# Linear attention and an MLP in one kernel: v in whole rows, x sums on another engine, and two transposes moved to DMA

## The chip, the cores and the metric

The kernel runs on one core of a Trainium2 chip. The metric is the device time in microseconds (us), the median of the runs.

## The reference

For 8 batches, 8 heads, 576 tokens and a head size of 64, the kernel computes a linear attention and, on its result, a normalised MLP with a residual:

```
q_s = softmax(q over the head size);  k_s = softmax(k over the tokens)
kv  = k_s^T v                       (64 x 64 per head)
x   = q_s kv, heads side by side    (8 x 576 x 512)
xn  = (x - mean) / sqrt(var + 1e-6) * g
out = x + relu(xn w1) w2            (w1 512 x 2048, w2 2048 x 512)
```

Inputs and output are float32.

## The kernel before, in words

**Chunks.** The tokens are worked in nine chunks of 512. Chunks 0 to 7 are the first 512 tokens of each batch; chunk 8 (C9) gathers the last 64 of all batches. Within a chunk a partition holds four consecutive tokens (T = 4), so "token 2" of a chunk means the third of each partition, a tile of 128 tokens. All matrix operands are bf16.

**Order.** The order of the work is written by hand. `mlp_steps` gives a chunk's MLP as a list of single matmuls with weights: 1 for one of 512 columns, 0.5 for one of 256. `run` goes through it and puts in side work (the next chunk's attention, the loads, the sums) at positions counted in these weights; a chunk from 2 on has 112. An engine runs its own instructions strictly in that order, and semaphores join the engines. SyncE (SP) issues the loads of q and k and the DMA transposes, GpSimd (POOL) those of v and the stores.

**Attention of a chunk.** ScalarE takes exp of q and k (L171 to L203). q's result is transposed by DMA (`eq_T`, L253; batch 1's on TensorE, L864). `kv_all` (L321) multiplies exp(k) with v, 32 matmuls for the first 512 tokens and 8 for the rest, and `kv_out` scales the result on VectorE (L330, L332). v stands in `vm`, one buffer for even and one for odd batches, with a column of ones beside each head. `load_v` brings v of batches 1 to 3 as one DMA in rows of four tokens into the tile `vt`, from which VectorE copies it into `vm` (`cast_v`, L131, in two halves); for batches 4 to 7 four DMAs go straight into `vm`, one per token (L144). Then `po_mm` (L358) makes x for one token tile, `x_fast` on VectorE scales it (L388) and centres it into xn (L380), and ScalarE sums the squares (L372).

**xn turned.** For the MLP, xn has to be transposed: by DMA in two halves of two tokens (`xn_T`, L253), in chunks 0 and 1 on TensorE (`xn_pT`, L864) with a copy on ScalarE (L866) or VectorE (L868).

**MLP.** Chunk 0 and chunk 1's first matrix product are plain matmuls (L456 for parts of a chunk, L441 for a whole one, L501 for the second product). Everything after uses Strassen's scheme with seven products in place of eight, for which sums have to be made: of w1 and w2 once, of xn per chunk (`sum_x`, L245; on GpSimd, but on VectorE for chunk 8 and for one sum of chunk 7), and of the hidden layer (`sum_h`, L532, on VectorE, four sums in two halves). The first product (`mm1_fast`, L693) does four groups, two at a time. Of each, the products come in the order 1, 5, 6, 2, 7, 3, 4, each first for the one group and then for the other. ScalarE seeds bank c from bank x after product 1 (L717) and copies bank b to `s` after product 5 (L721); VectorE adds x and s into b after product 6 (L724), and adds x and s into the hidden layer after product 7 (L727), from the bank x to which product 4 then adds. The second product (`mm2_fast`, L548) has seven products of 16 matmuls; VectorE gives the output (L559; plain chunks L472), GpSimd stores it (L565).

**Positions.** In chunks 2 to 6 the first half of the first three h sums stand at 30, 33 and 41: the adds L724 of the second pair of groups come at 40, L727 at 48.

Of the kernel before, what the change touches and what calls it, by code (L numbers as in the profile page):

```python
# [20 lines left out]
def kernel(  # L21
# [16 lines left out]
    nc = tc.nc  # L38
# [13 lines left out]
    VW = D + 1  # L52
    C9 = B
    FAST = 1
    CAST = (1, 2, 3)
    T0 = S // 64
    assert SR == 64 and B % 2 == 0 and S % 64 == 0

# [67 lines left out]

    vts = {}

    def cast_v(b, j):
        hs = slice(4 * j, 4 * j + 4)  # L130
        nc.vector.tensor_copy(  # L131
            out=vm[:, b % 2, :, hs, 0:D].rearrange("p t h d -> p h t d"), in_=vts[b][:, hs]
        )

    def load_v(b):

        if b in CAST:
            vts[b] = mlp.tile([P, H, T, D], BF16, tag="tq", name="vt", bufs=1)
            nc.gpsimd.dma_start(
                vts[b].rearrange("p h t d -> p h (t d)"), main_src(v, b, 0, H)  # L140
            )
        src = v[b, :, 0:SM, :].rearrange("h (p t) d -> p t h d", t=T)
        for t in range(0 if b in CAST else T):
            nc.gpsimd.dma_start(vm[:, b % 2, t, :, 0:D], src[:, t])  # L144
        for half in range(2):
            hs = slice(4 * half, 4 * half + 4)
            nc.gpsimd.dma_start(
                vr[SR * half : SR * half + SR, b % 2, hs, 0:D],
                v[b, hs, SM:S, :].transpose([1, 0, 2]),
            )  # L150
# [82 lines left out]
    def sum_x(c, i):  # L233

        if i == 0:
            tqs[c] = mlp.tile([P, 4, 2, 2, P], BF16, tag="tq", name="tq", bufs=1)
        (b11, b12), (b21, b22) = [
            [xnTs[c][:, 2 * half : 2 * half + 2, 2 * kh : 2 * kh + 2, :] for half in range(2)]
            for kh in range(2)
        ]  # L240
        t1, t2, t3, t4 = [tqs[c][:, n] for n in range(4)]
        dst, x, y = ((t1, b12, b11), (t2, b22, t1), (t3, b22, b12), (t4, b21, t2))[i]
        eng = nc.vector if c == C9 or (c == C9 - 1 and i == 1) else nc.gpsimd
        for t in range(2):
            eng.tensor_tensor(out=dst[:, t], in0=x[:, t], in1=y[:, t], op=ALU.subtract)  # L245

# [201 lines left out]
    def mm1_part(c, m, t0, tn, ko):  # L448

        if (m, t0, ko) == (0, 0, 0):  # L450
            new_h()
        half, at = divmod(t0, 2)
        if m % 2 == 0 and at == 0 and ko == 0:
            hbox["ph", m // 2] = mm_ps.tile([P, 2, 2, P], FP32, tag="m", name="ph")
        ph = hbox["ph", m // 2]
        nc.tensor.matmul(  # L456
            ph[:, m % 2, at : at + tn], (w1g if c else w1_sb)[:, ko, m * P : (m + 1) * P],
            xnTs[c][:, t0 : t0 + tn, ko, :],
            start=(ko == 0), stop=(ko == KO1 - 1),
        )  # L460
        if m % 2 == 1 and at + tn == 2 and ko == KO1 - 1:
            dst = hbox["h"][:, m - 1 : m + 1, 2 * half : 2 * half + 2]
            if c == 0 and half and (m // 2) % 2 == 1:
                nc.vector.tensor_scalar_max(dst, in0=ph, scalar1=0.0)
            else:
                nc.scalar.activation(dst, ph, AF.Relu)
# [283 lines left out]
    def mlp_steps(c):  # L750
        if c > FAST:
            return mm1_fast(c) + mm2_fast(c)
        full = range(KO2)
        first, parts = [], ()
        if c == 0:
            full = range(0)
            parts = ((0, 2, 0, 1), (0, 2, 1, 1), (2, 2, 0, 1), (2, 2, 1, 1), (4, 4, 0, 2), (0, 4, 2, 1),
                     (0, 4, 3, 1), (4, 4, 2, 2), (8, 4, 0, 2), (8, 4, 2, 2), (12, 4, 0, 2), (12, 4, 2, 2))
        else:
            full, parts = range(8, KO2), ((0, 8, 0, 2), (0, 8, 2, 2))  # L760
        for m0, mn, t0, tn in parts:
            first += [
                (0.25 * tn, lambda m=m, t0=t0, tn=tn, ko=ko: mm1_part(c, m, t0, tn, ko))
                for m in range(m0, m0 + mn) for ko in range(KO1)
            ]
        first += [(1, lambda m=m, ko=ko: mm1(c, m, ko)) for m in full for ko in range(KO1)]
        if c == 0:
            return first + [
                (1, lambda t=t, ko=ko: mm2_stream(c, t, ko))
                for n in range(4) for t in range(T) for ko in range(4 * n, 4 * n + 4)  # L770
            ]
        if c >= FAST:
            return first + mm2_fast(c)
        return first + [(1, lambda t=t, ko=ko: mm2(c, t, ko)) for t in range(T) for ko in range(KO2)]
# [25 lines left out]
    def prep_fast(b):  # L800

        s = [(57, lambda: exp_q(b, 0, 4)), (65, lambda: exp_q(b, 2, 4)), (79, lambda: eq_T(b))]
        s += [(81, lambda: exp_k(b, 0, 4)), (98, lambda: exp_k(b, 2, 4))]
        s += [(106, lambda: prep_kvrem(b))]
        return s

    def recip_q(c):
# [2 lines left out]
    def attn_fast(c):  # L810

        s = [(1, lambda: reduce_q(c, 0, 2)), (27, lambda: reduce_q(c, 2, 2)), (28, lambda: recip_q(c))]
        s += [(12, lambda: kv_all(c))]
        s += [(40, lambda: start_x(c))]
        for t, (p0, p1) in enumerate(((48, 53), (57, 59), (65, 67), (73, 75))):
            s += spread([lambda t=t, i=i: po_mm(c, t, i) for i in range(NP)], p0, p1)
            s += [(p1, lambda t=t: x_fast(c, t)), ((66, 74, 87, 91)[t], lambda t=t: square_sum(c, t))]
        s += [(61, lambda: xn_T(c, 0, 2)), (78, lambda: xn_T(c, 2, 2)), (95, lambda: rstd_op(c))]
        s += [((84, 100 if c == C9 - 1 else 88, 92, 101)[i], lambda i=i: sum_x(c, i)) for i in range(4)]
        return s  # L820

    def second_side():

        s = [(p, lambda i=i: quarter_w2(i, 1)) for i, p in enumerate((8.5, 13, 44, 46))]
        s += [(8.0, lambda: xn_pT(1, 3, nc.vector))]
        s += [(3, lambda: exp_q(2, 0, 4)), (7, lambda: exp_q(2, 2, 4)), (7.2, lambda: eq_T(2))]
        s += [(42, lambda: square_sum(1, 2)), (67, lambda: square_sum(1, 3)), (71, lambda: rstd_op(1))]
        s += [(7.3, lambda: load_batch(3, (2,), eqTs[2][0:1, T - 1, NP - 1, 0:4])), (31, lambda: load_batch(3, (0,)))]
        s += [(9 + 2 * j, lambda j=j: cast_v(2, j)) for j in range(2)]
        s += [(7.4, lambda: load_v(3))]  # L830
        s += [(93 + j, lambda j=j: cast_v(3, j)) for j in range(2)]
        s += [(15 + 3 * t, lambda t=t: reduce_q(2, t, 2)) for t in (0, 2)]
        s += [(36, lambda: recip_q(2))]
        s += [(18, lambda: exp_k(2, 0, 4)), (22, lambda: exp_k(2, 2, 4)), (26, lambda: prep_kvrem(2))]
        s += [(41, lambda: kv_all(2))]
        s += [(46, lambda: start_x(2))]
        for t, (p0, p1) in enumerate(((52, 54), (57, 59), (62, 65), (70, 74))):
            s += spread([lambda t=t, i=i: po_mm(2, t, i) for i in range(NP)], p0, p1)
            s += [(p1, lambda t=t: x_fast(2, t)), ((73, 82, 88, 94)[t], lambda t=t: square_sum(2, t))]
        s += [(60, lambda: xn_T(2, 0, 2)), (77, lambda: xn_T(2, 2, 2)), (100, lambda: rstd_op(2))]  # L840
        s += [(75, lambda: exp_q(3, 0, 4)), (79, lambda: exp_q(3, 2, 4)), (85, lambda: eq_T(3))]
        s += [(97, lambda: exp_k(3, 0, 4)), (108, lambda: exp_k(3, 2, 4)), (113, lambda: prep_kvrem(3))]
        s += [(p, lambda i=i: sum_w1(i, 1)) for i, p in ((3, 30),)]
        s += spread([lambda i=i: sum_x(2, i) for i in range(4)], 95, 108)
        return s
# [184 lines left out]
    with tc.manual_schedule(  # L1030
# [10 lines left out]
        def po_x(c, t):  # L1041
# [26 lines left out]
            + [(p, lambda i=i: sum_w1(i, 1)) for i, p in enumerate((96, 98, 100))]  # L1068
            + [(103 + 0.4 * j, lambda j=j: cast_v(1, j)) for j in range(2)]
            + [(104.5, lambda: prep_kvrem(1))]  # L1070
            + [(105, lambda: kv_mm(1, range(T))), (106, lambda: (kv_mm(1, range(T, T + 1)), kv_out(1), start_x(1)))]
            + [(111, lambda: po_x(1, 0)), (113, lambda: po_x(1, 1))]
            + [(116, lambda: po_x(1, 2)), (118, lambda: xn_pT(1, 0, nc.scalar)), (119, lambda: square_sum(1, 0))]
            + [(119.5, lambda: po_x(1, 3)), (123, lambda: xn_pT(1, 1, nc.scalar)), (124, lambda: square_sum(1, 1))]
            + [(128, lambda: xn_pT(1, 2, nc.scalar))]

        )
        for c in range(1, B):
# [12 lines left out]
            if c == B - 2:  # L1091
                side += [(1, load_qrem)]
                side += spread([lambda r=r: exp_qrem(r) for r in range(T)], 58, 80)
                side += [(84, lambda: eq_T(C9))]
            sums = [(57, 0)] if c == FAST else [(p, i) for i, p in enumerate((30, 41) if c == B - 1 else (30, 33, 41))]
            run(mlp_steps(c), side + [(at, lambda i=i: sum_h(0, i)) for at, i in sums])
        run(mlp_steps(C9), [(33 + 3 * i, lambda i=i: sum_h(0, i)) for i in range(2)])

# [29 lines left out]
```

## Time and profile before

| | us |
|---|---|
| runs | 266.63, 266.06, 266.3; median 266.3 |
| the profiled execution's own time | 266.63 |
| its span, first to last instruction | 264.8 |
| busy: TensorE, VectorE, ScalarE, GpSimd | 257.6, 217.0, 175.1, 90.4 |

The 1.8 us between the execution's time and its span lie outside the instructions. A chunk from 2 on takes some 26.3 us: chunk 3 begins its first product at 103.7, chunk 4 at 130.1, chunk 5 at 156.5, chunk 6 at 183.2, chunk 7 at 209.4 (timeline of TensorE). In a timeline line stand the start, the time until the last end, the engine, the line and operation, the tiles written and read, their sizes and how many instructions are drawn together; in square brackets the idle time ahead of it and who ended it. Ends of matmuls are modelled, and some instructions overlap on their engine, so the starts say more than the durations. A few records are missing: a jump of just one matmul in the starts is no wait.

### The profile page before, as it was taken

To read this page: it belongs to the slowest core of one execution; us is meant where nothing else is said; L and a number is where in the kernel's file an instruction comes from. 1 tells how busy PE (TensorE), PEld (TensorE's weight loads), DVE (VectorE), ACT (ScalarE), POOL (GpSimd) and SP (SyncE) were. 2 spreads that over 40 slices of the span, in tenths; PEclk is the share of its full clock that TensorE was granted. 3 is DMA by queue.
4 is the path that set the end of the run, shared out by engine and by line. 5 is a ranking of instruction groups with operands and counts; after the bars stand their busy time and mean duration, and the time that the engine had idled before them with its cause. 6 is when DMAs were issued, how large, how long until landed. Compare 5 with 4: busy or idle time off the path is not lost. (4 is left out here: it accounts for less than half of the span.)

```text
span 264.8 us, 6827 instructions
## 1 busy us (share of the span) xinstructions
PE 257.6 (97%) x2708; PEld 217.5 (82%) x2711; DVE 217.0 (82%) x465; ACT 175.1 (66%) x346; POOL 90.4 (34%) x144
## 2 busy tenths in 40 slices
PE   8999999999999999999999999999999999999993
PEld 5778755775988998889888988998899888888882
DVE  4577697968989996999699968996999789877873
ACT  4467851996966886678667866886678378438400
POOL 8742216303059208900880049307300800030000
PEclk9999999999999999999999999999999999999999
DMA  7999999987987995899789997997804530512014
GB/s 226 252 205 207 342 209 329 262 132 255 184 149 221 291 139 101 222 286 143 98 243 268 125 113 235 294 126 155 257 5 84 120 118 5 78 80 81 0 42 119
DMA packets 82328, 45.01 MB, mean 170 GB/s; under 512 B 58036, under 2 KB 78520, under 8 KB 82296
## 3 DMA queue, kind: packets, MB, share of 16 engines
q0 software_dynamic: 32800, 22.29, 45.8%
q1 hardware_dynamic: 48896, 21.76, 40.5%
q10 hardware_dynamic: 600, 0.53, 0.6%
q8 instruction: 21, 0.34, 0.5%
q14 instruction: 11, 0.09, 0.1%
HBM read 36.70 MB, written 9.44 MB: 174 GB/s over the span
## 5 line engine op out<-in xcount | busy, mean ns | idle before, releaser
L548 PEld LDWEIGHTS <-hs 128*128 128x128 bf16 x512 | 49.5, 98 | 5.7
L693 PEld LDWEIGHTS <-w_q 128*128 128x128 bf16 x448 | 43.0, 98 | 6.4 <-issue 1.1
L245 POOL TENSOR_TENSOR tq<-xnT 128x256 bf16<-128x256 bf16 x24 | 15.6, 665 | 76.6 <-DMA xnT<-xn 76.6
L548 PEld LDWEIGHTS <-hT 128*128 128x128 bf16 x384 | 37.2, 98 | 4.4
L693 PEld LDWEIGHTS <-w1g 128*128 128x128 bf16 x336 | 32.2, 98 | 3.9
L548 PE MATMUL ba<-w_q,hs 128*128 128x256 bf16 x256 | 31.7, 273 | 0.0
L693 PE MATMUL bx<-tq,w_q 128*128 128x256 bf16 x224 | 29.4, 272 | 0.2 <-ACT s L721 0.2
L372 ACT ACTIVATE scrap<-x,mv 128x512 bf16<-128x512 bf16 x36 | 25.9, 719 | 1.7 <-DVE x L388 1.3
L717 ACT COPY bc<-bx 128x512 f32<-128x512 f32 x28 | 15.2, 594 | 16.8 <-PE bx L693 16.8
L388 DVE SCALAR_TENSOR_TENSOR x<-po,rq 128x512 bf16<-128x512 f32 x34 | 23.3, 685 | 2.4 <-PE po L358 2.3
L565 POOL DMA_DIRECT2D out_dram<-ot x28 | 15.4, 556 | 24.1 <-DVE ot L559 24.0
L735 ACT ACTIVATE hT<-bc 128x512 bf16<-128x512 f32 x28 | 15.3, 595 | 12.4 <-PE bc L693 12.4
L207 DVE TENSOR_REDUCE zq<-eq 128x16 f32<-128x1024 bf16 (+1 forms) x20 | 20.6, 1049 | 2.0 <-ACT eq L198 2.0
L532 DVE TENSOR_TENSOR hs<-hT 128x1024 bf16<-128x1024 bf16 x32 | 21.3, 674 | 0.9 <-ACT hT L735 0.5
L724 DVE TENSOR_TENSOR bb<-bx,s 128x512 f32<-128x512 f32 x28 | 18.2, 694 | 4.1 <-ACT s L721 4.0
L735 ACT ACTIVATE hT<-bb 128x512 bf16<-128x512 f32 x28 | 15.2, 595 | 9.2 <-PE bb L693 9.2
L358 PE MATMUL po<-kv_sb,eqT 128*128 128x128 bf16 x120 | 20.5, 219 | 0.0
L727 DVE TENSOR_TENSOR hT<-bx,s 128x512 bf16<-128x512 f32 x28 | 18.0, 685 | 2.8 <-PE bx L693 2.8
L573 ACT COPY s<-ba 128x512 f32<-128x512 f32 x15 | 8.7, 579 | 12.5 <-PE ba L548 7.8
L548 PE MATMUL ba<-w_sb,hT 128*128 128x256 bf16 x128 | 16.7, 273 | 0.0
L548 PE MATMUL bb<-w_q,hs 128*128 128x256 bf16 x128 | 16.6, 273 | 0.0
L501 PE MATMUL pc<-w_sb,hT 128*128 128x512 bf16 x61 | 15.8, 379 | 0.2
(135 smaller groups left out, 541.1 us busy)
## 6 DMA issues: line engine op xcount, KB each, us to landing
out_dram<-ot POOLq DMA_DIRECT2D x32, 256.0 KB, 5.6
qt<-in_q_dram SPq DMA_DIRECT2D x5, 1024.0 KB, 6.3
kt<-in_k_dram SPq DMA_DIRECT2D x5, 1024.0 KB, 12.8
w_sb<-in_moe_w_ch_dram POOLq DMA_DIRECT2D x4, 512.0 KB, 16.4
qt<-in_q_dram POOLq DMA_DIRECT2D x2, 1024.0 KB, 14.6
kt<-in_k_dram POOLq DMA_DIRECT2D x2, 1024.0 KB, 14.5
vm<-in_v_dram POOLq DMA_DIRECT2D x16, 128.0 KB, 13.2
w_raw<-in_moe_w_ch_dram POOLq DMA_DIRECT2D x3, 512.0 KB, 12.8
```

Source lines behind the costliest of these rows:

```text
L207: nc.vector.reduce_sum(eqs[c][1][:, ts], eqs[c][0][:, ts], axis=AX.X)
L245: eng.tensor_tensor(out=dst[:, t], in0=x[:, t], in1=y[:, t], op=ALU.subtract)
L358: nc.tensor.matmul(pobox["p"][:, i * P : i * P + P], eqTs[c][:, t, i, :], kv_sb[:, c, i, :], start=True, stop=True,)
L372: nc.scalar.activation(scrap, x[:, t], AF.Square, bias=mv[:, t, 0:1], scale=-float(DM), accum_out=mv[:, t, 1:2],)
L388: nc.vector.scalar_tensor_tensor(x[:, t].rearrange("p (h d) -> p h d", h=H), in0=pobox[c, t].rearrange("p (h d) -> p h d", h=H), scalar=1. ...
L501: nc.tensor.matmul(hbox["pc", t], hbox["h"][:, ko, t, :], w2_sb[:, ko, :], start=(ko == 0), stop=(ko == KO2 - 1),)
L532: nc.vector.tensor_tensor(out=dst, in0=x, in1=y, op=op)
L548: nc.tensor.matmul(hbox[bank][:, t], lhsT, rhs, start=first and (own or t == 0) and k == 0, stop=k == KH - 1, skip_group_check=True)
L693: nc.tensor.matmul(dst[:, q], lhsT, rhs, start=first and q == 0 and ko == 0, stop=ko == 1, skip_group_check=True)
L724: nc.vector.tensor_tensor(out=at[g, "b"], in0=at[g, "x"], in1=at[g, "s"], op=ALU.add)
L727: nc.vector.tensor_tensor(out=h_out(g, 1, 1), in0=at[g, "x"], in1=at[g, "s"], op=ALU.add)
L735: nc.scalar.activation(h_out(g, odd, half), at[g, name], AF.Relu)
```

## The change

v of every batch from 1 on is now loaded as one DMA into `vt`, which has a buffer of its own (before, it shared one with the x sums). For batches 4 to 7 VectorE copies the first half into `vm` at position 94.5 and ScalarE the second at 107, in the chunk two before their own. All x sums of chunk 7 are on VectorE, at position 100. In chunk 1, tokens 2 and 3 of xn are transposed by DMA at chunk 0's position 125, and no longer on TensorE; for this x of token 3 comes ahead of the output of token 1, and the first product works 12 of 16 blocks of hidden columns on tokens 0 and 1 alone, before it takes up tokens 2 and 3 (before: 8 of 16). The kv product of batch 1 is no longer split around a matmul and stands at 106. In chunks 2 to 6 the h sums move from 30, 33, 41 to 30, 40.5, 42.

```diff
-    CAST = (1, 2, 3)
...
-    def cast_v(b, j):
+    def cast_v(b, j, eng=None):
         hs = slice(4 * j, 4 * j + 4)
+        dst = vm[:, b % 2, :, hs, 0:D].rearrange("p t h d -> p h t d")
+        if eng is nc.scalar:
+            nc.scalar.copy(dst, vts[b][:, hs])
+        else:
+            nc.vector.tensor_copy(out=dst, in_=vts[b][:, hs])
...
     def load_v(b):
-        if b in CAST:
-            vts[b] = mlp.tile([P, H, T, D], BF16, tag="tq", name="vt", bufs=1)
-            nc.gpsimd.dma_start(
-                vts[b].rearrange("p h t d -> p h (t d)"), main_src(v, b, 0, H)
-            )
-        src = v[b, :, 0:SM, :].rearrange("h (p t) d -> p t h d", t=T)
-        for t in range(0 if b in CAST else T):
-            nc.gpsimd.dma_start(vm[:, b % 2, t, :, 0:D], src[:, t])
+        vts[b] = mlp.tile([P, H, T, D], BF16, tag="vt", name="vt", bufs=1)
+        nc.gpsimd.dma_start(vts[b].rearrange("p h t d -> p h (t d)"), main_src(v, b, 0, H))
...
-        eng = nc.vector if c == C9 or (c == C9 - 1 and i == 1) else nc.gpsimd
+        eng = nc.vector if c >= C9 - 1 else nc.gpsimd
...
-            start=(ko == 0), stop=(ko == KO1 - 1),
+            start=(ko == 0 and m % 2 == 0 and at == 0), stop=(ko == KO1 - 1),
+            skip_group_check=True,
...
-            full, parts = range(8, KO2), ((0, 8, 0, 2), (0, 8, 2, 2))
+            full, parts = range(12, KO2), ((0, 12, 0, 2), (0, 12, 2, 2))
...
+        s += [(94.5, lambda: cast_v(b, 0)), (107, lambda: cast_v(b, 1, nc.scalar))]
...
-        s += [((84, 100 if c == C9 - 1 else 88, 92, 101)[i], lambda i=i: sum_x(c, i)) for i in range(4)]
+        s += [(100 if c == C9 - 1 else (84, 88, 92, 101)[i], lambda i=i: sum_x(c, i)) for i in range(4)]
...
-        s += [(8.0, lambda: xn_pT(1, 3, nc.vector))]
...
-            + [(105, lambda: kv_mm(1, range(T))), (106, lambda: (kv_mm(1, range(T, T + 1)), kv_out(1), start_x(1)))]
+            + [(106, lambda: (kv_all(1), start_x(1)))]
             + [(111, lambda: po_x(1, 0)), (113, lambda: po_x(1, 1))]
-            + [(116, lambda: po_x(1, 2)), (118, lambda: xn_pT(1, 0, nc.scalar)), (119, lambda: square_sum(1, 0))]
-            + [(119.5, lambda: po_x(1, 3)), (123, lambda: xn_pT(1, 1, nc.scalar)), (124, lambda: square_sum(1, 1))]
-            + [(128, lambda: xn_pT(1, 2, nc.scalar))]
+            + [(115.3, lambda: po_x(1, 2)), (118.5, lambda: xn_pT(1, 0, nc.scalar)), (119, lambda: square_sum(1, 0))]
+            + [(118, lambda: po_x(1, 3)), (123, lambda: xn_pT(1, 1, nc.scalar)), (124, lambda: square_sum(1, 1))]
+            + [(125, lambda: xn_T(1, 2, 2))]
...
-            sums = [(57, 0)] if c == FAST else [(p, i) for i, p in enumerate((30, 41) if c == B - 1 else (30, 33, 41))]
+            sums = [(57, 0)] if c == FAST else [(p, i) for i, p in enumerate((30, 41) if c == B - 1 else (30, 40.5, 42))]
```

## The prediction

> **What bounds the kernel now.** I read the page's busy line and clock row first, then who waited for whom on TensorE, then the timelines of TensorE and VectorE around the few waits.
>
> ```profile
> PE 257.6 (97%) x2708; PEld 217.5 (82%) x2711; DVE 217.0 (82%) x465; ACT 175.1 (66%) x346; POOL 90.4 (34%) x144
> PEclk9999999999999999999999999999999999999999
> ```
>
> TensorE is busy for 97% at full clock, and the chain that ended last is TensorE alone from 211 us on. So a change counts only if it takes work from TensorE, takes away one of its waits, or adds one. A busy PE is not yet PE at its peak: the waits show in the starts. Back to back, a 256-column matmul starts every 0.109 us, a 512-column one every 0.216, a 128-column one every 0.055, from groups in the timeline. Starts later than that after 25 us, beyond single lost records, are these: two around the first kv product (at 41.5 and 43.8), one in chunk 3 and one in chunk 4 (114.5, 140.9), two at the start of chunk 5 (157.2, 158.2) and two at the start of chunk 7 (210.1, 210.7). The waits of TensorE and one of the timeline's groups:
>
> ```profile
> PE bx L693 <- ACT s L721: 0.2, 1, 0.2
> PE bb L693 <- DVE ot L559: 0.2, 1, 0.2
> ```
>
> ```profile
> 140.57 1.20 PE L693 MATMUL bx<-tq,w_q 128*128 128x256 bf16 x8
> ```
>
> The view counts only what is idle by modelled ends (0.2 each), so the starts must be used: 1.20 us for eight matmuls, where 1.04 is usual.
>
> **Part 1: chunk 0's end.** TensorE before (timeline):
>
> ```profile
> 41.50 0.88 PE L321 MATMUL pkv<-vm,ek 128*64 128x65 bf16 x32
> 42.30 0.39 PE L501 MATMUL pc<-w_sb,hT 128*128 128x512 bf16 x1
> ...
> 42.87 1.25 PE L501 MATMUL pc<-w_sb,hT 128*128 128x512 bf16 x4
> 44.11 0.38 PE L358 MATMUL po<-kv_sb,eqT 128*128 128x128 bf16 x4
> ...
> 49.12 0.39 PE L864 MATMUL ptr<-ident,xn 128*128 128x128 bf16 x4
> 49.34 1.91 PE L456 MATMUL ph<-xnT,w1g 128*128 128x256 bf16 x16
> ```
>
> The kv product is no longer split and starts one 512-column matmul later, at 41.72, when VectorE's second copy of v (ends 41.68) is there. Its 40 matmuls take 0.75 (chunk 1's, 58.59 to 59.34), so they end at 42.47; kv_out takes 1.2 from there (before: 42.87 to 44.06) and po starts at 43.74, not 44.11: **-0.37**. Eight transposes on TensorE go (L864, 0.22 per four): -0.44. Sixteen 512-column matmuls become 32 of 256: 16 x 0.003 = +0.05. Together **-0.39**. ScalarE and VectorE each lose a copy of 0.4 to 0.6 that nobody waited for.
>
> In return TensorE now waits for a DMA. Chunk 1 starts at 49.12 - 0.37 = 48.75 and works 48 matmuls (48 x 0.1094 = 5.25) on tokens 0 and 1; it needs tokens 2 and 3 at 54.0. VectorE's chain of x: x_fast of token 0 at 44.53 - 0.37 = 44.16, then 1.0 per token and 0.66 for the one output that stays between them, so token 3's xn ends at 48.90. SP issues 0.16 later (as after 147.28 and 200.08), at 49.06. SP waits for that and holds behind it only eqT of batch 2, which isn't ready before some 51.7. How long the transpose takes is the open term; L253's rows:
>
> ```profile
> L253 SPq DMA_TRANSPOSE xnT<-xn x14: 1232/1396/3487, 65.3 to 228.3; - x14
> DMA to landing us min/median/max: 3.1/4.3/9.6
> 49.00:53.00 4.00, 4.00 (x42) 3.53 (x40) 3.70 (x9) 4.00 (x8) 1.54 (x3) 1.00 1.13 274
> ```
>
> Issue to landing is 3.1 to 3.8 where the DMA engines are empty (200.2, 202.5, 223.9, 228.3), 5.0 and 6.8 where v is still landing (94.5, 147.4), 9.6 behind k in its own queue (65.3). The last line (stretch, engines' busy time, clock, DMA share, GB/s) shows 49 to 53 us full: 113% DMA share, 274 GB/s, with batch 2's v and four stores. eqT, twice the size, took 6.6 there from 52.5. I take the mean of 5.0, 6.6 and 6.8, 6.1: landing at 55.2, a wait of **+1.2**. Ends: 0 (3.1 to 4.9) and +4.7 (9.6).
>
> The Trainium skill (Advanced Engine Details and Errata, X-Bar Transpose (TRN2)) says transposing DMAs on this chip run as fast as ordinary ones. By it the 256 KB would be there before 54.0 and the term be 0, the first rival below. The rows agree with it only where the engines are empty.
>
> **Part 2: v of batches 4 to 7.** GpSimd issues one DMA instead of four (0.9 against 3.6 us), in rows four times as long. Nobody on TensorE waited for v itself. The copies are new work: VectorE 0.42 each (L131's row) at a place where it idles 1.54 per chunk (before `bb` L576, waiting for ScalarE's s); ScalarE at most 1.06 (L171, as many elements) in an idle 2.03 before L717. Both are covered: 0. The new flags of the matmuls (start, skip_group_check) cost nothing that a row shows. v must be there for the copy, or VectorE's queue stands still: before, it landed by 151.9 in the worst chunk, the copy comes at 152.3, and fewer packets make it earlier. Uncovered, VectorE's 1.1 and ScalarE's 1.0 us of slack would have to be exceeded first. What may be gained is chunk 4's late x transposes (6.8 beside v): GpSimd's x sums started at 156.1 with chunk 5 at 156.5, and TensorE lost 0.13 + 0.38 = **-0.51** (0 if the lateness isn't v's).
>
> **Part 3: chunk 7's x sums.** GpSimd's start at 206.0 and VectorE's own share waits for them and is slow:
>
> ```profile
> 206.69 1.42 DVE L245 TENSOR_TENSOR tq<-xnT,tq 128x256 bf16<-128x256 bf16 x2 [1.48 <-POOL tq L245]
> 231.82 0.48 DVE L245 TENSOR_TENSOR tq<-xnT 128x256 bf16<-128x256 bf16 x2
> ```
>
> With GpSimd at work two take 1.42, without it 0.48 (0.40 start to start). Eight on VectorE are 4 x 0.40 = 1.6 from 205.95, done at 207.55, where VectorE was free at 208.04 before. Its outputs come 0.49 earlier, so the two banks that TensorE waited for (0.09 + 0.34, released by `ot` L559) are free in time: **-0.43**.
>
> **Part 4: order of VectorE in chunks 2 to 6.** The second h sum (L532) moves from ahead of the two adds L724 to behind them. Chunk 5, VectorE, then TensorE:
>
> ```profile
> 165.14 0.63 DVE L532 TENSOR_TENSOR hs<-hT 128x1024 bf16<-128x1024 bf16 x1
> 165.80 0.69 DVE L532 TENSOR_TENSOR hs<-hs,hT 128x1024 bf16<-128x1024 bf16 x1
> 166.41 1.29 DVE L724 TENSOR_TENSOR bb<-bx,s 128x512 f32<-128x512 f32 x2
> 167.61 0.68 DVE L532 TENSOR_TENSOR hs<-hT 128x1024 bf16<-128x1024 bf16 x1
> 168.21 1.28 DVE L727 TENSOR_TENSOR hT<-bx,s 128x512 bf16<-128x512 f32 x2
> ```
>
> ```profile
> 165.68 1.04 PE L693 MATMUL bx<-tq,w_q 128*128 128x256 bf16 x8
> ...
> 169.40 1.04 PE L693 MATMUL bx<-tq,w1g 128*128 128x256 bf16 x8
> ```
>
> L724 can't start before ScalarE's copy s, 0.73 after TensorE's 165.68 (in chunk 8, with no sum ahead of it, 0.72). Before, the sum filled that wait. Now VectorE idles 0.6 there, and the sum stands ahead of L727: 166.41 + 4 x 0.60 = 168.81 for its first half, 169.41 for the second. The product at 169.40 (the last one, into bank x) adds to the bank that L727 reads. TensorE follows an add by 0.75 from the add's start (114.02 to 114.77): 169.56 instead of 169.40, then its second group at 170.16 instead of 169.56 + 0.44 = 170.00. That is 0.16 + 0.16, with rounding 0.33 a chunk, five times 1.65. In return the waits on L724 in chunks 3 and 4 go (2 x 0.19): **+1.27**. Ends: -0.38 if L727 is never late, +1.65.
>
> **Sum** against the profiled execution (266.63; span 264.8): -0.37 - 0.39 + 1.2 - 0.51 - 0.43 + 1.27 = +0.77, 267.4. That execution is 0.33 above the median of the three, 266.3, and the sum goes on the median: **267.1**.
>
> **Rivals.** *In time:* the transpose lands by 54.0. For it: 3.1 to 3.8 in empty stretches. Against: the full stretch. 267.1 - 1.2 = 265.9. *No wait at L727,* the faster side: VectorE reaches L727 early enough, or the product doesn't queue on it. It decides if the adds start 0.3 earlier than ScalarE's row allows. Against: that row, in chunks 5, 6 and 8 alike. Then the h sum's move is a gain: 267.1 - 1.65 = 265.4, and 264.2 with the transpose in time. *Very late transpose:* like 9.6 at 65.3; eqT and q of batch 3 follow it. 267.1 + 3.5 = 270.6; 268.9 at half of that. The Trainium skill (TensorE: Matmul & The Clock Gate, What's actually happening) has the clock halve after an idle window of about 3.4 us; that would add some 1.7 as an estimate from that page, and the clock row here, at 9 throughout, shows no such case. *v isn't on the path:* part 2 gives 0, 267.6, within the forecast's spread.
>
> **Numbers.** 0.2% is 0.53 us, about what a measurement can tell. Forecast (wait of 0.5 to 2.6): 0.50, 266.4 to 268.5. In time: 0.22, 265.3 to 266.4. No wait at L727: 0.16, 264.2 to 266.0. Very late: 0.12. Faster: most of the third, part of the second, 0.22; same 0.24; slower 0.54. Left out of the range are half of the third and most of the last: 265.0 to 268.9.
>
> **What would show it.** SP's first transpose at 49 and where TensorE's 49th matmul of chunk 1 starts (55 right, 54 wrong); in chunks 2 to 6 the last product of the second half 0.16 later than its predecessor allows, released by L727, and VectorE idle 0.6 ahead of L724; chunk 5 and 7 without a gap at their start; po of chunk 1 at 43.7. Wrong if the transpose takes below 5 us, or L727 starts within 2.6 us of the start of the product whose result L724 adds (now 2.5; 3.1 expected).

## The result, and the profile after

The changed kernel takes 268.15 us (median of 10 runs, 266.93 to 269.22); the kernel before took 266.37 beside it (10 runs, 266.06 to 266.82). The ratio is 1.0061, with a 95% interval of 1.0045 to 1.0077: slower by 1.2 to 2.1 us. The forecast of 267.1 had the sign; it was 1.05 too low, inside the 266.4 to 268.5 given for it. The runs of the changed kernel lie further apart than those before (2.3 us against 0.8), and its profiled execution, 269.22 with a span of 267.2, is the longest of the ten. So the differences below are placed with the trace, and priced with the experiments' medians.

In code lines, what stood at L456, L501, L321, L358, L253, L245, L532, L548, L559, L693, L721, L724 and L727 now stands at L451, L497, L316, L353, L248, L240, L528, L544, L555, L689, L717, L720 and L723. The page's busy line and clock row:

```profile
PE 258.5 (97%) x2719; PEld 218.9 (82%) x2719; DVE 217.6 (81%) x474; ACT 179.7 (67%) x349; POOL 75.8 (28%) x126
PEclk9999999999999999999999999999999999999999
```

TensorE is still the bound, at full clock; nothing was won or lost by the clock. GpSimd lost 14.6 us of work, and DMA many small packets (under 512 bytes 42516, before 58036); what that is worth the experiments tell. TensorE's longest wait, then its place in the timeline:

```profile
PE ph L451 <- DMA xnT<-xn: 1.5, 1, 1.5
```

```profile
53.32 1.36 PE L451 MATMUL ph<-xnT,w1g 128*128 128x256 bf16 x11
56.14 3.88 PE L451 MATMUL ph<-xnT,w1g 128*128 128x256 bf16 x34 [1.46 <-DMA xnT<-xn]
```

The last matmul on tokens 0 and 1 starts at 54.41, the first on tokens 2 and 3 at 56.14: 1.63 more than the usual 0.11. SP's timeline, and the rows of this one transpose (L248, starts 48 to 51):

```profile
49.45 1.36 SPq L248 DMA_TRANSPOSE xnT<-xn  x1
52.20 5.60 SPq L248 DMA_TRANSPOSE eqT<-eq  x1
62.01 0.38 SPq L114 DMA_DIRECT2D qt<-in_q_dram  x1
```

```profile
  PE ph L451: 1.5, 1
...
DMA to landing us min/median/max: 6.6/6.6/6.6
```

Issued at 49.45, landed at 56.09: 6.64. A second thing stands in SP's rows: q of batch 3 is loaded at 62.01, where it was 59.40 before, since eqT of batch 2 (52.20) now takes 9.56 instead of 6.60. The lateness goes on to the transposes of x of chunk 2 and to GpSimd's sums of them, and TensorE meets it at chunk 2's start (timelines of TensorE and GpSimd):

```profile
78.83 1.04 PE L689 MATMUL bx<-xnT,w1g 128*128 128x256 bf16 x8
79.93 1.33 PE L689 MATMUL bb<-tq,w_q 128*128 128x256 bf16 x8
81.18 0.93 PE L689 MATMUL bx<-tq,w_q 128*128 128x256 bf16 x7
```

```profile
78.58 1.30 POOL L240 TENSOR_TENSOR tq<-xnT 128x256 bf16<-128x256 bf16 x2 [13.39 <-DMA xnT<-xn]
```

Eight such matmuls need 0.87 from start to start of the next group; here it is 1.10 and 1.25. That is 0.61 us, in three gaps of 0.22, 0.30 and 0.09, which the sum of the prediction does not have. Chunk 5, VectorE and then TensorE, with the h sum behind the two adds:

```profile
168.46 1.30 DVE L720 TENSOR_TENSOR bb<-bx,s 128x512 f32<-128x512 f32 x2 [0.69 <-ACT s L717]
169.67 0.68 DVE L528 TENSOR_TENSOR hs<-hs,hT 128x1024 bf16<-128x1024 bf16 x1
170.27 0.69 DVE L528 TENSOR_TENSOR hs<-hT 128x1024 bf16<-128x1024 bf16 x1
170.87 1.28 DVE L723 TENSOR_TENSOR hT<-bx,s 128x512 bf16<-128x512 f32 x2
```

```profile
171.36 0.22 PE L353 MATMUL po<-kv_sb,eqT 128*128 128x128 bf16 x1
171.61 1.20 PE L689 MATMUL bx<-tq,w1g 128*128 128x256 bf16 x8
```

VectorE idles 0.69 ahead of L720, comes to L723 at 170.87, and TensorE's last product starts 0.74 behind that, at 171.61. By the starts it loses 0.15 to 0.20 ahead of the product and 0.16 inside it, in each of chunks 2 to 6.

Where the 2.24 us between the two last matmuls lie, from starts on TensorE in the two profiled executions:

| from, to | before | after | difference |
|---|---|---|---|
| span's start to the first second product of chunk 0 (L501) | 31.53 | 32.12 | +0.59 |
| to po of chunk 1 | 12.58 | 12.15 | -0.43 |
| to the start of chunk 1 | 5.23 | 5.01 | -0.22 |
| to the kv product of batch 3, in chunk 2 | 30.81 | 32.86 | +2.05 |
| to the kv product of batch 7, in chunk 6 | 105.73 | 106.11 | +0.38 |
| to the last matmul | 74.53 | 74.40 | -0.13 |

The first row is not the change's: in the other kernels that stretch came out from 31.41 to 31.99, and in the changed kernel's execution TensorE was already late by 0.47 at its first transposes of q (7.71 against 7.24), ahead of all that the change touches. The fourth is 1.63 + 0.61 less four transposes (0.22). The fifth holds four of the five late L723 (1.30) less the gaps of before (0.91: 0.20 each in chunks 3 and 4, and chunk 5's start), which gives 0.39. The sixth holds the fifth L723 (+0.31) and chunk 7's start (-0.42).

The two executions' own times differ by 2.59, and 0.35 of that lies behind the last matmul: 0.16 up to the end of the span, and 0.19 outside the span. The 0.19 is no accident of one execution. The time outside the span is 1.93 to 2.03 us in all ten runs of the changed kernel, and 1.74 to 1.86 in those of the kernel before that ran beside the experiments. Of the kernels below, e1_sums_back, e2_tensor_transposes and e3_both_back keep it (1.98 to 2.00 on average); those with one or two parts alone don't have it (1.78 to 1.81). What makes it is not shown; no term of the prediction stood for it.

### The profile page after: what moved, and what is told of

Same layout as the page of the kernel before. It is cut to its first block, busy times and chain, and to the rows that moved or that the text cites. A ratio compares the mean times of both kernels' runs of the same rounds, so it can differ in the third digit from the quotient of the medians.

```text
span 267.2 us, 6837 instructions
## 1 busy us (share of the span) xinstructions
PE 258.5 (97%) x2719; PEld 218.9 (82%) x2719; DVE 217.6 (81%) x474; ACT 179.7 (67%) x349; POOL 75.8 (28%) x126
## 2 busy tenths in 40 slices
DMA packets 70903, 45.26 MB, mean 169 GB/s; under 512 B 42516, under 2 KB 67096, under 8 KB 70872
## 4 chain that ended last, share of the span: by engine, by line
PE 68%; DVE 0%; issue 0%
PE bx L689 19%; PE ba L544 18%; PE bb L689 9%; PE bc L689 5%; PE bb L544 5%; PE be L544 5%; PE bc L544 5%; PE po L353 2%; PE pkv L316 1%; PE po L360 1%; PE bd L544 0%; DVE yl L584 0%; DVE zq L202 0%
## 5 line engine op out<-in xcount | busy, mean ns | idle before, releaser
L544 PEld LDWEIGHTS <-hs 128*128 128x128 bf16 x512 | 49.5, 98 | 5.7
L689 PEld LDWEIGHTS <-w_q 128*128 128x128 bf16 x448 | 43.0, 98 | 5.6 <-issue 0.3
L544 PEld LDWEIGHTS <-hT 128*128 128x128 bf16 x384 | 37.1, 98 | 4.4
L689 PEld LDWEIGHTS <-w1g 128*128 128x128 bf16 x336 | 32.3, 98 | 5.3 <-issue 1.0
L240 POOL TENSOR_TENSOR tq<-xnT 128x256 bf16<-128x256 bf16 x20 | 12.9, 661 | 79.3 <-DMA xnT<-xn 60.2
L544 PE MATMUL ba<-w_q,hs 128*128 128x256 bf16 x256 | 31.7, 273 | 0.0
L689 PE MATMUL bx<-tq,w_q 128*128 128x256 bf16 x224 | 29.0, 273 | 0.0
L720 DVE TENSOR_TENSOR bb<-bx,s 128x512 f32<-128x512 f32 x28 | 18.2, 694 | 6.6 <-ACT s L717 6.4
L528 DVE TENSOR_TENSOR hs<-hT 128x1024 bf16<-128x1024 bf16 x32 | 21.3, 674 | 0.7 <-ACT hT L731 0.5
L353 PE MATMUL po<-kv_sb,eqT 128*128 128x128 bf16 x120 | 20.5, 219 | 0.0
L723 DVE TENSOR_TENSOR hT<-bx,s 128x512 bf16<-128x512 f32 x28 | 18.0, 684 | 3.0 <-PE bx L689 3.0
L462 ACT ACTIVATE hT<-ph 128x512 bf16<-128x512 f32 x24 | 14.0, 597 | 6.2 <-PE ph L451 6.2
L569 ACT COPY s<-ba 128x512 f32<-128x512 f32 x15 | 8.7, 578 | 12.5 <-PE ba L544 7.8
L544 PE MATMUL ba<-w_sb,hT 128*128 128x256 bf16 x128 | 16.7, 273 | 0.0
L544 PE MATMUL bb<-w_q,hs 128*128 128x256 bf16 x128 | 16.6, 273 | 0.0
```

Source lines behind the costliest of these rows:

```text
L353: nc.tensor.matmul(pobox["p"][:, i * P : i * P + P], eqTs[c][:, t, i, :], kv_sb[:, c, i, :], start=True, stop=True,)
L528: nc.vector.tensor_tensor(out=dst, in0=x, in1=y, op=op)
L544: nc.tensor.matmul(hbox[bank][:, t], lhsT, rhs, start=first and (own or t == 0) and k == 0, stop=k == KH - 1, skip_group_check=True)
L689: nc.tensor.matmul(dst[:, q], lhsT, rhs, start=first and q == 0 and ko == 0, stop=ko == 1, skip_group_check=True)
L720: nc.vector.tensor_tensor(out=at[g, "b"], in0=at[g, "x"], in1=at[g, "s"], op=ALU.add)
L723: nc.vector.tensor_tensor(out=h_out(g, 1, 1), in0=at[g, "x"], in1=at[g, "s"], op=ALU.add)
```

## The experiments

Two groups take the change apart, and a third asks why the transpose is late. Each is compared with the kernel before on its own chip.

**Undoing parts.** Three runs give back the h sums, the two transposes, and both; a fourth puts the h sums alone into the kernel before.

```diff
-... (30, 41) if c == B - 1 else (30, 40.5, 42))]
+... (30, 41) if c == B - 1 else (30, 33, 41))]
```

> The changed kernel with the h sums of chunks 2 to 6 back at 30, 33, 41. If the sum behind the adds is what makes TensorE wait for L727, the five pairs of waits (0.15 + 0.17) go and the time falls by 1.2 to 1.6, to about 266.8. If v's copies or the loads are the cost, it stays at 268.1.

Measured (`e1_sums_back`): 266.75, ratio 1.0017 [1.0005, 1.0028]. The waits on L723 are gone; the one in chunk 1 stays.

```diff
-            full, parts = range(12, KO2), ((0, 12, 0, 2), (0, 12, 2, 2))
+            full, parts = range(8, KO2), ((0, 8, 0, 2), (0, 8, 2, 2))
...
+        s += [(8.0, lambda: xn_pT(1, 3, nc.vector))]
...
-            + [(125, lambda: xn_T(1, 2, 2))]
+            + [(128, lambda: xn_pT(1, 2, nc.scalar))]
```

> The changed kernel with chunk 1's tokens 2 and 3 transposed on TensorE again, in the order of before (the kv product stays in one piece). If the late DMA transpose costs, the wait of 1.6 in chunk 1 and the 0.6 at the start of chunk 2 go and 0.39 of TensorE's work comes back: about 266.4. If the wait only hides another one close behind it, it stays above 267.5.

Measured (`e2_tensor_transposes`): 266.98, ratio 1.0023 [1.0014, 1.0031], 0.6 above the theory's time and clearly below the rival's. There is no wait in chunk 1 or at chunk 2's start, eqT of batch 2 takes 6.44 (before 6.60), and TensorE waits 0.15 and 0.16 on L723 in all five chunks.

> Both undone; v in whole rows, the two copies of v, chunk 7's x sums on VectorE and the kv product in one piece stay. Two causes that add up: 268.15 - 1.2 - 1.8 = 265.2, faster than before by 1.2 (kv 0.37, chunk 7's start 0.43, chunk 5's start up to 0.5). If v's new copies cost, it ends at 266.4 or above.

Both edits together (`e3_both_back`): 265.38, ratio 0.9966 [0.9956, 0.9975], **faster than both kernels**, by 0.9 us than before. In its timeline the last product into bank x follows the po matmul ahead of it by 0.06, not by 0.25:

```profile
168.33 0.22 PE L353 MATMUL po<-kv_sb,eqT 128*128 128x128 bf16 x1
168.39 1.04 PE L689 MATMUL bx<-tq,w1g 128*128 128x256 bf16 x8
```

From 45 us on, no start in it is late by 0.08 or more for another engine.

> The kernel before with only the h sums moved, to 30, 40.5, 42. Wait for L727: 5 x 0.33 less 0.38 for the waits that go in chunks 3 and 4 = +1.2, 267.6. If the move only pays (adds L724 in time) it is 266.0; if neither is on the path 266.4.

Measured (`e4_sums_only`): 267.53, ratio 1.005 [1.0037, 1.0064]. In chunk 5 the line of the same product reads

```profile
169.81 0.22 PE L358 MATMUL po<-kv_sb,eqT 128*128 128x128 bf16 x1
170.01 1.19 PE L693 MATMUL bx<-tq,w1g 128*128 128x256 bf16 x8
```

So the four fit together. The h sums cost 1.33 us alone (0.50% of 266.3), and the difference of the ratios gives 1.2 (changed kernel against the first) and 1.5 (the second against the third). The DMA transposes cost 1.0 (changed kernel against the second) to 1.4 (the first against the third). What is left of the change gains 0.9, although it keeps the 0.19 outside the span.

**Parts alone, in the kernel before.** Chunk 7's x sums:

```diff
-        eng = nc.vector if c == C9 or (c == C9 - 1 and i == 1) else nc.gpsimd
+        eng = nc.vector if c >= C9 - 1 else nc.gpsimd
```

> The kernel before with one part of the change alone: all of chunk 7's x sums on VectorE at position 100. Theory (the two late banks at chunk 7's start, 0.09 and 0.34 us, go, and nothing else changes): -0.43, ratio 0.9984, about 265.9. Rival (VectorE's 1.6 us of added work delay something else by as much, or the gap is closed further on): 0, 266.3. The gap at 210 us in TensorE's starts tells which.

Measured (`c7_only`): 265.88, ratio 0.9983 [0.9973, 0.9994], that is -0.45 us. TensorE at chunk 7's start, first before and then with this edit:

```profile
210.34 0.61 PE L693 MATMUL bb<-tq,w_q 128*128 128x256 bf16 x4
211.12 0.60 PE L693 MATMUL bb<-tq,w_q 128*128 128x256 bf16 x4 [0.17 <-DVE ot L559]
```

```profile
209.37 1.04 PE L693 MATMUL bx<-xnT,w1g 128*128 128x256 bf16 x8
210.25 1.04 PE L693 MATMUL bb<-tq,w_q 128*128 128x256 bf16 x8
```

One group of eight where two of four were, 0.88 after the group ahead of it: both gaps are gone. The larger one, 0.33, stands in every trace that leaves these sums as before (before, v_only, kv_only, e4_sums_only).

v in whole rows, for batches 4 to 7:

```diff
+        vts[b] = mlp.tile([P, H, T, D], BF16, tag="vt", name="vt", bufs=1)
+        nc.gpsimd.dma_start(vts[b].rearrange("p h t d -> p h (t d)"), main_src(v, b, 0, H))
...
+        s += [(94.5, lambda: cast_v(b, 0)), (107, lambda: cast_v(b, 1, nc.scalar))]
```

> The kernel before with one part of the change alone: v of batches 4 to 7 in whole rows and copied by VectorE and ScalarE. Theory (the copies are covered, and the gaps of 0.13 and 0.38 us at chunk 5's start go, since they came from the slow transposes of x beside v in chunk 4): -0.5, ratio 0.998, about 265.8. First rival (the gaps weren't v's): 0, 266.3. Second rival (the copies delay VectorE or ScalarE where TensorE waits for them): slower by 0.3 or more, 266.6 and up, with new waits in chunks 2 to 5 near positions 94 to 110.

Measured (`v_only`): 266.51, ratio 1.0008 [1.0, 1.0017]: no gain, at most a small loss, and no new wait in the trace. The mechanism is there all the same. The rows of the x transpose that starts at 147 in chunk 4, before and with this edit:

```profile
DMA to landing us min/median/max: 6.8/6.8/6.8
```

```profile
DMA to landing us min/median/max: 3.5/3.5/3.5
```

Other traces with whole rows have 3.57 (e3_both_back), 3.06 (e2_tensor_transposes) and 4.75 (first_dummy). But with v loaded as before, the same transpose took 6.42 (kv_and_c7), 5.92 (c7_only), 5.83 (kv_only) and 5.11 (e4_sums_only) in other profiled executions. At chunk 5's start the first of these lost 0.10, the other three nothing. TensorE there, before, and in c7_only:

```profile
156.47 1.04 PE L693 MATMUL bx<-xnT,w1g 128*128 128x256 bf16 x8
157.46 1.03 PE L693 MATMUL bb<-tq,w_q 128*128 128x256 bf16 x8
158.71 1.03 PE L693 MATMUL bx<-tq,w_q 128*128 128x256 bf16 x8 [0.22 <-ACT s L721]
```

```profile
156.65 1.04 PE L693 MATMUL bx<-xnT,w1g 128*128 128x256 bf16 x8
157.52 1.04 PE L693 MATMUL bb<-tq,w_q 128*128 128x256 bf16 x8
158.39 1.04 PE L693 MATMUL bx<-tq,w_q 128*128 128x256 bf16 x8
```

The steps are 0.87 with v untouched. So the loss of 0.51 us was that of the one execution in five in which the transpose was latest; at 6.42 it is 0.10, and from 5.92 down nothing.

The kv product of batch 1 in one piece:

```diff
-            + [(105, lambda: kv_mm(1, range(T))), (106, lambda: (kv_mm(1, range(T, T + 1)), kv_out(1), start_x(1)))]
+            + [(106, lambda: (kv_all(1), start_x(1)))]
```

> The kernel before with one part of the change alone: the kv product of batch 1 in one piece at chunk 0's position 106. Theory (the step of the prediction): po of chunk 1 starts 0.37 us earlier after the product's start and nothing else changes: ratio 0.9986, about 265.9. Rival (the product of the rest waits for ScalarE's exp of k and VectorE's second copy of v all the same, so a product that starts one matmul later waits less but ends no sooner): 0 to -0.1, 266.2 to 266.3.

Measured (`kv_only`): 266.17, ratio 0.9999 [0.9985, 1.0013]. In the trace the step is right: from the first L501 to po of chunk 1 it takes 12.14 us. Kernels with the product in one piece show 12.14 to 12.35 there (first_dummy alone, with a transfer added ahead, 13.33), those with it split 12.58 to 12.84. But this execution began that stretch 0.46 later than the one of before (31.99 against 31.53), and the interval of the whole, -0.40 to +0.35, neither shows the 0.37 nor rules it out.

> The kernel before with the kv product of batch 1 in one piece and chunk 7's x sums on VectorE, v's loads as before: the version of the DMA transposes and h sums taken back, without the new loads and copies of v. If v's part is worth nothing, it takes the same as that version: 265.4, ratio 0.9966. If v's copies cost the 0.2 us that v alone showed (1.0008), it takes 265.2, ratio 0.9959. If v's loads gain in most executions, 265.7 or more.

Measured (`kv_and_c7`): 265.49, ratio 0.9978 [0.9968, 0.9989], -0.59 us. Against c7_only's 0.9983 the kv product adds 0.1; against e3_both_back's 0.9966, which also has v's part, v would add 0.3, where alone it gave nothing. The intervals overlap in both cases. That v gains a little together with the rest, by taking away small waits on L724 that come and go between executions (none above 0.07 in v_only, e1_sums_back and e3_both_back, one of 0.15 here, two or three of 0.10 to 0.17 in before, kv_only and c7_only), is argued and not shown.

**Why the transpose is late.** Three theories: it shares the DMA engines with the load of batch 2's v and of the rest of its k and v (issued from 42.6, landed by 53.4), or with chunk 0's stores, or it is slow as the first of the program. First the stores of tokens 1 to 3 held back to chunk 1's position 30:

```diff
+        if c == 0 and t:
+            held.append((t, ot))
...
+        s += [(30, stores_0)]
```

> The changed kernel with the stores of chunk 0's tokens 1 to 3 held back to chunk 1's position 30, behind the DMA transposes. If these stores are what slows the transposes, x of tokens 2 and 3 lands within 5 us, TensorE's wait of 1.6 falls to under 0.5, eqT of batch 2 lands before 60 and chunk 2's start loses its 0.6: about 266.3. If v's loads slow them, or the first transpose is slow by itself, the wait stays above 1 and the time near 268.

Measured (`e5_stores_late`): 267.79, ratio 1.0067 [1.0043, 1.0091]. xn's transpose still takes 6.55 and TensorE waits 1.54. But eqT behind it (L248, starts 51 to 55) takes 5.5, and chunk 2 starts without a gap; in the changed kernel the same row reads 9.6:

```profile
DMA to landing us min/median/max: 5.5/5.5/5.5
```

```profile
DMA to landing us min/median/max: 9.6/9.6/9.6
```

So without the three stores eqT is not late, and without xn's transpose ahead of it, but with the stores, it isn't either (6.44). From chunk 1's start to the last matmul it is 212.71 in this trace against 213.37, mostly the 0.61 of chunk 2's start. The medians (267.79 and 268.15, ratios with overlapping intervals) don't resolve that, the less as this kernel lacks the 0.19 outside the span (1.80).

Then that load of batch 2 moved behind eqT's transpose:

```diff
-        load_behind(2)
+        load_behind(2, (2, 0))
...
+        s += [(7.35, lambda: (load_v(2), load_krem(nc.gpsimd, 2)))]
```

> The changed kernel with the load of v (and of k and v of the rest) of batch 2 moved from chunk 0 to behind the DMA transpose of eqT of batch 2, so that no load of v is under way while xn of chunk 1's tokens 2 and 3 is transposed (49 to 56 us); its copies and v of batch 3 come later too. Theory 'full engines' (the 6.6 us come from sharing the DMA engines with v of batch 2): issue to landing falls to 3.1 to 4.5 us and TensorE's wait in chunk 1 goes (under 0.2 us). Rival 'slow here anyway' (the transpose is as long for a reason of its own, such as being the first one of the program): it stays at 6 to 6.6 us and the wait at 1.2 to 1.6 us. One look; the whole time is not used, since the later loads may cost elsewhere.

One execution (`v2_late`), 282.5 us, as v itself now comes late. The row of xn's transpose (starts 48 to 51) and TensorE over the place of the wait:

```profile
L248 SPq DMA_TRANSPOSE xnT<-xn x1: 1333/1333/1333, 49.0 to 49.0; - x1
...
DMA to landing us min/median/max: 3.9/3.9/3.9
```

```profile
52.76 5.18 PE L451 MATMUL ph<-xnT,w1g 128*128 128x256 bf16 x46
```

It took 3.9 us, with the stores of the same stretch under way and still as the first transpose of the program; TensorE runs through 46 matmuls without a stop. So the load of batch 2's v and rests is the cause. And eqT (51.75) takes only 6.25 here, with xn's transpose ahead of it and the stores under way: it takes the load, that transpose and the stores together to make it 9.56.

> The changed kernel with one more DMA transpose of 128 KB, of chunk 0's first token tile into a spare tile that nobody reads, issued by SyncE at position 90 of chunk 0 (about 37 us), so that the one of xn of chunk 1 at 49 us is no longer the first of the program. Theory 'full engines': xn's transpose still takes 6.0 to 6.7 us and TensorE waits 1.2 to 1.6 us. Rival 'the first one is slow': xn's takes 3 to 4.5 us and the wait goes, while the added one is long for its size (over 4 us). One look; the time should be that of the changed kernel, 267 to 269.

```diff
+    spare = const.tile([P, NP, P], BF16)
...
+                (90, lambda: nc.sync.dma_start_transpose(spare, xs[0][2][:, 0])),
```

One execution (`first_dummy`), 269.68 us: inconclusive. The added transpose did not run at 37 us but at 14.4, as soon as its data was there, since nothing stood ahead of it in SP's queue; there it took 9.0 beside the weights' loads. All of chunk 1 came about 1 us later. xn's transpose was issued 2.8 us before v had landed (3.2 in the changed kernel), took 5.16, between the two forecasts, and TensorE waited 0.14.

Last, a remedy: all 16 blocks of hidden columns on tokens 0 and 1 first.

```diff
-            full, parts = range(12, KO2), ((0, 12, 0, 2), (0, 12, 2, 2))
+            full, parts = range(0), ((0, 16, 0, 2), (0, 16, 2, 2))
```

> The changed kernel with all 16 blocks of hidden columns worked on tokens 0 and 1 before tokens 2 and 3 are taken up, 1.75 us more work ahead of the wait. If only the landing counts, the wait falls by 1.75, to near 0, and chunk 2's start by none: about 266.6. If the transpose is slowed by what TensorE's progress sets off (ScalarE, loads), it lands later too and 0.5 or more is left.

Measured (`e6_all_blocks_first`): 268.47, ratio 1.0077 [1.0049, 1.0105]. The wait in chunk 1 is gone, and the time isn't. eqT still takes 8.95, and TensorE stops before and in chunk 2's start instead (timeline):

```profile
75.97 1.91 PE L544 MATMUL ba<-w_q,hT 128*128 128x256 bf16 x16 [0.68 <-ACT s L569]
77.72 1.04 PE L689 MATMUL bx<-xnT,w1g 128*128 128x256 bf16 x8
79.18 0.61 PE L689 MATMUL bb<-tq,w_q 128*128 128x256 bf16 x4 [0.43 <-DVE ot L555]
```

ScalarE, whose copy (L569) the first of these stops waits for, had itself stood 0.95 us for k of batch 3, and VectorE, whose outputs (L555) the second waits for, 3.23 us for its v (2.11 in the changed kernel). The wait for xn had covered part of that: with it gone, TensorE meets the late batch 3 earlier. Two things are late behind this transpose, and hiding one of them was worth nothing here.

## Why the prediction was right in sign and 1.05 us too low

**Kv product in one piece (-0.37): right at its place.** It is -0.43 in the table. What of it reaches the total is not settled (0.0 and 0.1 in two experiments, with intervals that hold 0.37).

**Eight transposes (-0.39): right as far as it shows.** It is -0.22 ahead of chunk 1; the four inside it are not seen apart from the waits there.

**The wait for the DMA (+1.2): mechanism right, a little short.** It was 1.63, 1.19 and 1.54 in three traces (changed kernel, e1_sums_back, e5_stores_late), with 6.64, 6.20 and 6.55 to landing instead of 6.1. "Where v is still landing" was the right class of rows, and v2_late shows it to be the cause. The rule of the Trainium skill that I had set against it (Advanced Engine Details and Errata, X-Bar Transpose (TRN2): transposing DMAs as fast as ordinary ones) about holds here: an ordinary store of 256 KB issued at 50.38 beside it took 5.95, the transpose 6.64. What was wrong was to draw a wait of 0 from it; ordinary DMAs are slow in that stretch too (without v's load, in v2_late, the same store took 3.48).

**What was left out: eqT and what follows it (+0.61 in the trace).** The prediction named this chain, but only for a transpose of 9.6 us (*Very late transpose*). It needs no such thing: a transpose of 6.64 ahead of eqT, with v's load and the stores beside it, makes eqT 9.56. What TensorE loses by it at chunk 2's start differs from trace to trace: 0.61 here, 0.12 in e1_sums_back (eqT 8.78), 1.61 in first_dummy (eqT 8.91). "SP holds behind it only eqT of batch 2" was read as harmless, because eqT's issue hardly moves (52.54 to 52.20). Its landing moved by 2.6.

**v of batches 4 to 7: the copies at 0 were right, the gain of 0.51 was wrong.** This is the step that failed. v did slow the transposes of x, and whole rows do cure that (6.8 to 3.5); but the 0.51 at chunk 5's start belonged to one execution, and the sum then took this loss of an execution of 266.63 off the median of 266.3. The prediction gave "0 if the lateness isn't v's" as the other end; the lateness was v's, and the end was near 0 because the 5.1 to 5.9 us of most executions is in time. v alone measured 1.0008.

**Chunk 7's x sums (-0.43): right**, -0.45 alone, with both gaps gone.

**The h sum behind L724 (+1.27): right**, in place, size and cause: 0.15 to 0.20 and 0.16 a chunk where 0.16 and 0.16 were forecast, and 1.33 alone.

Put together: what is not sums or DMA transposes was forecast at -1.31 (with -0.51 in it) and measured at -0.9 (with the 0.19 outside the span in it); the DMA transposes at 1.2 - 0.39 = +0.81 and measured at 1.0 to 1.4, the more by what follows eqT; the sums at +1.27 and measured at 1.2 to 1.5. The three together hold the 1.05; the intervals don't divide it more finely. That 268.15 still fell inside 266.4 to 268.5 is in part luck: this width was given for the wait alone, which was off by some 0.4, and it happened to hold the other misses too.

## What to carry to other kernels

A gap seen in one profiled execution is worth its size only if it stands in others too; a wait that rests on when a DMA lands comes and goes, one that rests on the order of an engine's own work (L727, 0.15 to 0.20 in five chunks) stood in every trace with the sums moved. When a transfer is put ahead of another in one queue, the price is read at the landing of the second and of what waits for it, and not only at the wait for the first. And an instruction that fills another engine's latency (the h sum ahead of L724) is not free to move: behind the add it cost 0.3 us a chunk.

## What the runs showed of the hardware that was not expected

In v2_late TensorE stood still from 57.9 to 70.2. The stretches' lines (stretch, engines' busy time, clock, DMA share, GB/s):

```profile
58.00:62.00 4.00, 0.00 (x0) 0.00 (x0) 0.00 (x0) 0.36 (x1) 3.60 (x6) 1.00 0.54 161
62.00:63.00 1.00, 0.00 (x0) 0.00 (x0) 0.00 (x0) 0.00 (x0) 0.00 (x0) 0.76 0.89 301
63.00:70.00 7.00, 0.00 (x0) 0.00 (x0) 0.28 (x1) 0.00 (x0) 0.00 (x0) 0.50 1.27 252
...
73.00:76.00 3.00, 3.00 (x15) 2.11 (x14) 2.40 (x5) 0.76 (x3) 0.61 (x1) 0.50 1.06 134
76.00:78.00 2.00, 2.00 (x14) 0.95 (x12) 0.27 (x1) 1.19 (x2) 0.00 (x0) 0.96 0.99 94
```

The granted clock fell to half at about 62.5, some 4.6 us into the stop, and was back at about 76, some 6 us after work had resumed (with a stop of 1 us in between). Matmuls of 256 columns started every 0.213 us meanwhile instead of every 0.109. That is 5 us of work at half speed, so some 2.5 us lost, as an estimate. The Trainium skill (TensorE: Matmul & The Clock Gate, What's actually happening) gives windows of about 3.4 us that run freely. The 4.6 us fit that, if such a window has to lie wholly inside the stop. The prediction's 1.7 us, an estimate from that page, is less than the 2.5 here. The stops of up to 1.63 us in the changed kernel left the clock at 1.00.

The transpose of 512 KB, behind that of xn and beside four stores of 256 KB, took 9.56, without three of these stores 5.5, and with the stores but without batch 2's v 6.25. That of xn in the same stretch hardly changed without the stores (6.64 and 6.55), and fell to 3.9 without v. And a DMA that is given a place in the program runs when its queue reaches it: 14.4 instead of 37 us in first_dummy.
